# First expert layer by token halves, its weights by column halves, and two transfers of the second chunk moved

## The chip, the cores and the metric

The kernel runs on one core of one Trainium2 chip. The metric is the device time of the program in microseconds (us). Times are quoted as medians of all runs of a kernel, of the fast ones alone where one was slow. A ratio is the mean time of one kernel's fast runs over that of the other kernel's fast runs of the same rounds, so it is not quite the ratio of the medians. Positions in time below are in us from the start of the profiled span, which is some 1.7 us shorter than the time of the same run.

## The reference, cut to what matters

Four sequences of 768 tokens pass a gated linear attention with 8 heads of 48 channels. The result, 3072 rows of 384, passes four small two-layer experts whose outputs are mixed with given probabilities.

```python
state = np.zeros((B, H, D, D))
for t in range(S):
    state = f[:, :, t, :, None] * state + np.einsum('bhd,bhe->bhde', k[:, :, t], v[:, :, t])
    y[:, :, t] = np.einsum('bhd,bhde->bhe', q[:, :, t], state)
...
p = domain_probs / (domain_probs.sum(-1, keepdims=True) + 1e-09)
for e in range(E):                       # E = 4, w1: 384 x 1024, w2: 1024 x 384
    h = np.maximum(x @ w1[e], 0.0)
    out += p[:, e:e + 1] * (h @ w2[e])
```

## The kernel before

The sequence is cut into six chunks of 128 tokens, numbered c = 0 to 5 (the text also says "second chunk" for c = 1); a chunk holds 4 batches, so 512 rows of the expert part. All work is put down as small operations with an assumed cost for one or more engines, a priority number, dependencies, and the buffers they take and free. A planner in the kernel runs through assumed time and hands out operations; the order in which it hands them out is the order in which the instructions are emitted, on every engine and on the queue of SyncE (SP), which issues the loads of the chunks, small copies, transposing copies and the stores. An engine takes its instructions in this order. The assumed costs set orders; they are not measured times. An eviction, below, is the copy of a matmul's result out of a PSUM bank (PSUM is the memory into which the matmuls write) into a buffer in SBUF, the working memory; the kernel reuses the bank only after it.

```python
rooms = {"ps_m": 4, "ps_t": 4, "f": 4, "q": 4, "k": 4, "v": 4, ..., "xT": 2, "h": 2, "o": 6}   # buffers
...
def load(c, nm, b, n):                     # f, k, q, v of batches b .. b+n-1 of a chunk
    ins[c, nm, b] = nc.sync.dma_start(...)
    if (c, nm, b) == (1, "f", 0):
        after(ins[c, nm, b], ins["w", 5])  # behind the sixth of eight weights
def load_w(i, e, which):                   # one weight, f32 in memory, bf16 in SBUF
    ins["w", i] = nc.gpsimd.dma_start(out=w[:, e], in_=r[e])
    if i == 0:
        after(ins["w", 0], ins[0, "q", B - 1])
...
def mm_h(c, e, fc, n0, n1):                # first layer, 128 of 1024 hidden columns
    for kk in range(KD):                   # KD = 3
        nc.tensor.matmul(out=..., lhsT=w1_sb[:, e, kk, fc*128:(fc+1)*128], rhs=tl("xT", c)[:, kk, n0:n1], ...)
def ev_o(c, e, nt, part, cols, eng):       # output of one expert times its probability, into an "o" tile
...
for c in range(C):
    u0 = unit[0]                           # running number of expert units, used as priority
    if c == 0:
        zip_units(hl(c, 0, 0, NT, ALL), [])            # 8 units of 512 rows
    ...
    if c + 2 < C:
        for half in range(2):
            for j, nm in enumerate("fkqv"):
                add_load(c + 2, nm, 2 * half, 2, u0 + 30 + 4 * half + j, deps=[wd[5]])
```

In the head, until the first expert matmul, filler matmuls on a tile named busy keep TensorE active. In the profiles, the matmuls that read xT and w_sb are the first layer of the experts, those that read w_sb and h the second; qk, QK, AT, y, yb belong to the attention; o is an output tile.

## Time and profile before

| | before |
|---|---|
| time, three runs first measured | 303.52 us (303.27 to 303.71) |
| span of the profile | 301.9 us |
| TensorE busy | 96% |
| first expert matmul starts | 23.86 us |
| last matmuls end | 298.40 us |

TensorE bounds the kernel. The page and the chain that show it stand in the prediction below. To see where TensorE loses time although it is "busy", I compared start to start: for each kind of matmul there is an interval at which it repeats when nothing is waited for (0.2158 us for 512 columns of the first layer, 0.1093 for 256, 0.1623 for the 384 of the second layer, 0.0555 for a transpose, and so on). The sum of these intervals over the program's order is the nominal work; what the trace needs beyond it between two matmuls is lost there. For the kernel before, start 23.86 + nominal 272.04 + lost 2.24 = 298.14, the start of the last matmul. This account is used for every run below.

### The profile page before, as it was taken

The numbers are of one execution on the slowest core, as the hardware profiler recorded it, in microseconds if no ns is written. First come the engines' busy times: TensorE is split into PE (matmuls) and PEld (weight loads), VectorE is DVE, ScalarE is ACT, GpSimd is POOL, SyncE is SP. The second block draws the span as 40 slices with busy tenths as digits, with TensorE's granted clock in tenths as the row PEclk, the third lists the DMA queues.
The fourth block names the chain that finished last, engine by engine and source line by source line (L and its number), as shares of the span: only waits on it lengthen the run. The fifth ranks groups of instructions, "written<-read, shape, count | busy, mean of one in ns | idle before, by whom it ended". The sixth has DMA issues, their size and how long they took to land.

```text
span 301.9 us, 5498 instructions
## 1 busy us (share of the span) xinstructions
PE 291.2 (96%) x2107; PEld 168.6 (56%) x2137; DVE 130.1 (43%) x249; ACT 171.2 (57%) x302; POOL 95.5 (32%) x158
## 2 busy tenths in 40 slices
PE   7889999999999999999999999999999999999995
PEld 5654555566775566556555555555555555555553
DVE  5674002788752574506464335453415342201223
ACT  4766664755767454777356585445475444465430
POOL 4386300316576047423334533522342000000000
PEclk9999999999999999999999999999999999999999
DMA  9999999991995669989699969201322201200003
GB/s 150 203 168 207 208 208 205 179 157 34 197 228 119 117 121 181 213 155 158 125 199 173 207 122 154 48 16 37 91 60 51 49 15 40 78 0 2 0 0 104
DMA packets 134222, 36.08 MB, mean 120 GB/s; under 512 B 125340, under 2 KB 132636, under 8 KB 134196
## 3 DMA queue, kind: packets, MB, share of 16 engines
q1 hardware_dynamic: 128400, 29.40, 54.7%
q0 software_dynamic: 5760, 6.29, 12.5%
q8 instruction: 16, 0.26, 0.4%
q14 instruction: 10, 0.08, 0.1%
q10 hardware_dynamic: 36, 0.05, 0.1%
HBM read 31.51 MB, written 4.72 MB: 120 GB/s over the span
## 4 chain that ended last, share of the span: by engine, by line
PE 78%; DMA 12%; SPq 5%; POOL 2%; issue 1%; DVE 1%; POOLq 0%; DVEq 0%
PE ps_m L363 37%; PE ps_m L351 34%; DMA w_sb<-in_moe_w_dram 8%; SPq L225 5%; DMA q<-in_q_dram 4%; PE ps_t L307 2%; POOL w_sb L232 1%; PE ps_t L322 1%; PE ps_t L318 1%; PE ps_t L328 1%; POOL qk L283 1%; PE ps_t L259 1%; DVE qk L283 1%; PE ps_t L292 1%; PE ps_t L347 0%
## 5 line engine op out<-in xcount | busy, mean ns | idle before, releaser
L359 ACT ACTIVATE h<-ps_m 128x512 bf16<-128x512 f32 (+1 forms) x170 | 97.9, 577 | 99.4 <-PE ps_m L351 92.5
L363 PE MATMUL ps_m<-w_sb,h 128*128 128x384 bf16 x776 | 152.7, 324 | 0.2
L351 PE MATMUL ps_m<-xT,w_sb 128*128 128x512 bf16 (+1 forms) x594 | 150.2, 362 | 2.1 <-DMA w_sb<-in_moe_w_dram 0.7
L363 PEld LDWEIGHTS <-h 128*128 128x128 bf16 x776 | 73.4, 98 | 57.4
L370 DVE SCALAR_TENSOR_TENSOR o<-ps_m,pn,o 128x384 f32<-128x384 f32 (+1 forms) x73 | 44.6, 611 | 109.2 <-PE ps_m L363 104.9
L351 PEld LDWEIGHTS <-w_sb 128*128 128x128 bf16 x624 | 59.9, 98 | 47.1 <-DMA w_sb<-in_moe_w_dram 0.8
L283 POOL TENSOR_TENSOR qk<-q,e 128x384 bf16<-128x384 f32 x18 | 21.5, 1196 | 62.3 <-ACT e L269 33.4
L342 POOL TENSOR_TENSOR Sf<-Sf,egs 48x192 f32<-48x192 f32 x40 | 20.4, 511 | 45.4 <-DVE Sf L335 43.4
L357 DVE TENSOR_SCALAR h<-ps_m 128x512 bf16<-128x512 f32 (+1 forms) x38 | 21.5, 576 | 28.5 <-PE ps_m L351 27.1
L311 DVE TENSOR_TENSOR AT<-ps_t,mask 128x512 bf16<-128x512 f32 x48 | 30.2, 683 | 8.3 <-PE ps_t L307 8.3
L283 POOL TENSOR_TENSOR qk<-k,e 128x384 bf16<-128x384 f32 x21 | 22.1, 1052 | 18.2 <-ACT e L271 11.1
L269 ACT ACTIVATE e<-ps_t 128x384 f32<-128x384 f32 x20 | 17.3, 863 | 3.2 <-PE ps_t L259 1.4
L335 DVE TENSOR_TENSOR Sf<-Sf,ps_t 48x192 f32<-48x192 f32 x40 | 14.0, 349 | 10.7 <-PE ps_t L328 10.1
L372 ACT ACTIVATE o<-ps_m,pn 128x384 f32<-128x384 f32 x22 | 12.8, 580 | 4.2 <-PE ps_m L363 3.4
L343 POOL CAST sb<-Sf 48x192 bf16<-48x192 f32 x40 | 13.6, 340 | 2.6
L583 PE MATMUL ps_m<-busy 128*128 128x256 bf16 x61 | 12.4, 334 | 1.3 <-DVE busy L140 1.3
L251 ACT ACTIVATE ex<-f 128x768 f32<-128x768 f32 (+1 forms) x14 | 10.5, 750 | 4.1 <-DMA f<-in_f_logit_dram 4.0
L271 ACT ACTIVATE e<-ps_t 128x384 f32<-128x384 f32 x24 | 12.7, 531 | 0.0
L221 POOL CAST vb<-v 128x384 bf16<-128x384 f32 x19 | 9.8, 538 | 7.4 <-DMA v<-in_v_dram 5.1
L322 PE MATMUL ps_t<-vb,AT 128*128 128x48 bf16 x192 | 11.4, 184 | 0.7 <-ACT vb L219 0.7
L322 PEld LDWEIGHTS <-AT 128*128 128x128 bf16 x192 | 10.0, 97 | 2.8 <-issue 1.0
L255 ACT ACTIVATE gp<-ex 128x768 bf16<-128x768 f32 (+1 forms) x14 | 10.5, 750 | 0.4
(54 smaller groups left out, 131.6 us busy)
## 6 DMA issues: line engine op xcount, KB each, us to landing
w_sb<-in_moe_w_dram POOLq DMA_DIRECT2D x8, 768.0 KB, 18.5
out_dram<-o SPq DMA_DIRECT2D x23, 192.0 KB, 2.2
f<-in_f_logit_dram SPq DMA_DIRECT2D x10, 384.0 KB, 4.2
k<-in_k_dram SPq DMA_DIRECT2D x10, 384.0 KB, 5.0
q<-in_q_dram SPq DMA_DIRECT2D x10, 384.0 KB, 6.3
v<-in_v_dram SPq DMA_DIRECT2D x10, 384.0 KB, 5.8
f<-in_f_logit_dram SPq DMA_DIRECT2D x4, 192.0 KB, 4.3
k<-in_k_dram SPq DMA_DIRECT2D x4, 192.0 KB, 4.2
```

The costliest lines, as they stand in the source:

```text
L225: ins[c, nm, b] = nc.sync.dma_start(out=tl(nm, c, b // 2)[:, hh(b, n), :], in_=srcs[nm][c, :, b * H:(b + n) * H, :])
L269: nc.scalar.activation(out=e[:, 0].rearrange("t (d h) -> t h d", d=D), in_=cs[:, 0:HD].rearrange("t (i r d) -> t r i d", r=2, d=D), func=A ...
L283: engines[eng].tensor_tensor(out=tl("qk", c, b)[:, j, :, 0:D].rearrange("t (i r) d -> t i r d", r=2), in0=tl("qk"[j], c, b // 2)[:, hh(b), ...
L311: nc.vector.tensor_tensor(out=tl("AT", c, b)[:, r].rearrange("s i t -> s (i t)"), in0=tl("A", c, b, r).rearrange("s i t -> s (i t)"), in1= ...
L322: nc.tensor.matmul(out=y[:, h * D:(h + 1) * D], lhsT=AT[:, r, i, :], rhs=vb[:, h, :], start=(c == 0), stop=True, skip_group_check=True)
L335: nc.vector.tensor_tensor(out=Sf[rows, b], in0=Sf[rows, b], in1=KV[rows, :, r, :], op=ALU.add)
L342: nc.gpsimd.tensor_tensor(out=Sf[rows, b], in0=Sf[rows, b], in1=eg, op=ALU.mult)
L351: nc.tensor.matmul(out=tl("hp", c, e, fc, n0)[:, n0:n1], lhsT=w1_sb[:, e, kk, fc * 128:(fc + 1) * 128], rhs=tl("xT", c)[:, kk, n0:n1], sta ...
L357: nc.vector.tensor_relu(out=dst, in_=src)
L359: nc.scalar.activation(out=dst, in_=src, func=AF.Relu)
L363: nc.tensor.matmul(out=tl("op", c, e, nt, part)[:, cols], lhsT=tl("h", c, e)[:, fc, nt * T:(nt + 1) * T], rhs=w2_sb[:, e, fc, cols], start ...
L370: nc.vector.scalar_tensor_tensor(out=o, in0=op, scalar=pe, in1=o, op0=ALU.mult, op1=ALU.add)
```

## The change

The intent: the first expert's first layer need not wait for all four batches of chunk 0 nor for the whole weight, so TensorE starts earlier; and chunk 1's keys and queries come earlier because the last weight stands back. The costs that the planner assumes for chunk 0 are set anew. The core of the diff (cuts marked):

```diff
+        for o in self.ops:
+            if o.name.split(" ")[-1].startswith("0.") and set(o.costs) & {"ACT", "DVE"}:
+                o.lag += 0.1
...
-        if (c, nm, b) == (1, "f", 0):
-            after(ins[c, nm, b], ins["w", 5])
+        if (c, nm, b) == (1, "f", 1):
+            after(ins[c, nm, b], ins["w", w_gate])
-    def load_w(i, e, which):
+    def load_w(i, e, which, cols):
-        ins["w", i] = nc.gpsimd.dma_start(out=w[:, e], in_=r[e])
+        ins["w", i] = nc.gpsimd.dma_start(out=w[:, e, :, cols], in_=r[e][:, :, cols])
+        if i == w_gate + 2:
+            after(ins["w", i], ins[1, "k", 0])
...
+    add_load(1, "f", 0, 1, -980, cost=0.1)
+    pieces = [(0, 1, slice(0, F // 2)), (0, 1, slice(F // 2, F))] + [...]
+    wd, w_gate = {}, len(pieces) - 3
...
-            p, d, half = slot(b0, 0) - 0.5, 0.54 if gran == 1 else 0.84, b0 // 2
+            p, d, half = slot(b0, 0) - 0.5, 0.43 if gran == 1 else 0.84, b0 // 2
... (seven more assumed costs of chunk 0)
-            zip_units(hl(c, 0, 0, NT, ALL), [])
+            for n0, n1, xs in ((0, N2, LO), (N2, NT, HI)):
+                zip_units(hl(c, 0, n0, n1, xs), [])
```

More of the change, by code (lines that the diff above doesn't have):

```diff
@@ L381, with add_load @@
     ld = {}
-    nw = [(0, 1), (1, 1), (0, 2), (2, 1), (1, 2), (3, 1), (2, 2), (3, 2)]
-    def add_load(c, nm, b, n, prio, deps=()):
-        op = P.add(f"ld {nm}{c}.{b}", {"DMA": 1.05 * n}, lambda e: load(c, nm, b, n), prio,
+    def add_load(c, nm, b, n, prio, deps=(), cost=None):
+        op = P.add(f"ld {nm}{c}.{b}", {"DMA": cost or 1.05 * n}, lambda e: load(c, nm, b, n), prio,
                    deps=deps, takes=[(nm, c, b // 2)], lag=2.0)
@@ L392 @@
         add_load(0, x[0], int(x[1]), 1, -1000 + i)
-    wd = {}
-    for i, (e, which) in enumerate(nw):
-        iss = P.add(f"w issue {i}", {"POOL": 0.9}, lambda _, i=i, e=e, which=which: load_w(i, e, which),
-                    -500 + i, deps=[ld[0, "q", B - 1]])
-        wd[e, which] = wd[i] = P.add(f"w {i}", {"DMA": 4.5}, lambda _: None, -500 + (0, 1, 2, 3, 4, 5, 101.5, 103.5)[i], deps=[iss], lag=2.0)
-    for half in range(2):
-        for j, nm in enumerate("fkqv"):
-            add_load(1, nm, 2 * half, 2, -400 + 4 * half + j, deps=[wd[5]])
+    add_load(1, "f", 0, 1, -980, cost=0.1)
+    pieces = [(0, 1, slice(0, F // 2)), (0, 1, slice(F // 2, F))] + [
+        (e, which, slice(0, F if which == 1 else Din)) for e, which in ((1, 1), (0, 2), (2, 1), (1, 2), (3, 1), (2, 2), (3, 2))]
+    wd, w_gate = {}, len(pieces) - 3
+    for i, (e, which, cols) in enumerate(pieces):
+        if i == w_gate + 2:
+            for x in ((1, "f", 1, 1), (1, "k", 0, 2), (1, "q", 0, 2), (1, "v", 0, 2)):
+                add_load(*x, -430 + len(ld), deps=wd[3, 1])
+        iss = P.add(f"w issue {i}", {"POOL": 0.8}, lambda _, i=i, x=(e, which, cols): load_w(i, *x),
+                    -500 + i, deps=[ld[0, "q", B - 1]] + ([ld[1, "k", 0]] if i > w_gate + 1 else []))
+        op = P.add(f"w {i}", {"DMA": 2.25 if i < 2 else 4.5}, lambda _: None,
+                   -500 + (0, 0.5, 1, 2, 3, 4, 5, 6, 111)[i], deps=[iss], lag=1.5)
+        wd[e, which] = wd.get((e, which), []) + [op]
+    for x in ((1, "f", 2, 2), (1, "k", 2, 2), (1, "q", 2, 2), (1, "v", 2, 2)):
+        add_load(*x, -400 + len(ld), deps=wd[3, 1])
     xdone, kvdone = {}, {}
@@ L408, in attention @@
         for b0 in range(0, B, gran):
-            p, d, half = slot(b0, 0) - 0.5, 0.54 if gran == 1 else 0.84, b0 // 2
+            p, d, half = slot(b0, 0) - 0.5, 0.43 if gran == 1 else 0.84, b0 // 2
             g1 = P.add(f"gate1 {c}.{b0}", {"ACT": d}, lambda e, b0=b0: gate1(c, b0, gran), p,
-                       deps=[ld[c, "f", b0]], takes=[("ex", c, b0)], frees=[("f", c, half)])
+                       deps=[ld[c, "f", b0 + i] for i in range(gran)], takes=[("ex", c, b0)], frees=[("f", c, half)])
             g2 = P.add(f"gate2 {c}.{b0}", {"ACT": d}, lambda e, b0=b0: gate2(c, b0, gran), p + 0.1,
@@ L423, in attention @@
                        deps=[G[b]], takes=[pt_("cs")], lag=0.2, frees=[("gp", c, half)])
-            ex = P.add(f"exps {c}.{b}", {"ACT": 0.98 if c else 1.0}, on(exps), s(0) + 0.1, deps=[cs],
+            ex = P.add(f"exps {c}.{b}", {"ACT": 0.98 if c else 0.82}, on(exps), s(0) + 0.1, deps=[cs],
                        takes=[("e", c, b)] + ([("egs", c, b)] if c == 0 else []), frees=[pt_("cs")])
@@ L427, in attention @@
                             frees=[("e", c, b)], lag=2.0) if c and more else None)
-            pe = {"DVE": 0.55} if c == 0 and b == B - 1 else {"DVE": 0.55, "POOL": 1.36} if c == 0 else {"DVE": 0.6, "POOL": 1.0} if c == 1 else {"POOL": 1.0}
+            pe = {"DVE": 0.47} if c == 0 and b == B - 1 else {"DVE": 0.47, "POOL": 1.36} if c == 0 else {"DVE": 0.6, "POOL": 1.0} if c == 1 else {"POOL": 1.0}
             qm = P.add(f"q {c}.{b}", pe, one(product, 0), s(4) - 0.2,
@@ L432, in attention @@
                        deps=[ex, ld[c, "k", b]], takes=[("qk", c, b)], frees=[("k", c, half), ("e", c, b)])
-            vb = P.add(f"v {c}.{b}", {"ACT": 0.52} if c + b == 0 else {"ACT": 0.52, "DVE": 0.36} if c == 0 else {"POOL": 0.5, "ACT": 0.52} if c == 1 else {"POOL": 0.5}, one(cast_v), s(4),
+            vb = P.add(f"v {c}.{b}", {"ACT": 0.42} if c + b == 0 else {"ACT": 0.42, "DVE": 0.28} if c == 0 else {"POOL": 0.5, "ACT": 0.52} if c == 1 else {"POOL": 0.5}, one(cast_v), s(4),
                        deps=[ld[c, "v", b]], takes=[("vb", c, b)], frees=[("v", c, half)])
@@ L440, in attention @@
                 parts = [(slice(0, 2), [tq, tk])] if c or b < B - 1 else [(slice(j, j + 1), [tj]) for j, tj in enumerate((tq, tk))]
-                et = [P.add(f"ev_tp {c}.{b}", {"DVE": 0.69, "ACT": 1.05} if len(parts) == 1 else {"DVE": 0.37, "ACT": 0.55},
+                et = [P.add(f"ev_tp {c}.{b}", {"DVE": 0.69, "ACT": 1.05} if c else {"DVE": 0.6, "ACT": 0.92} if len(parts) == 1 else {"DVE": 0.35, "ACT": 0.49},
                             lambda e, b=b, js=js: copy(e, tl("QK", c, b)[0:MP, js], tl("tp", c, b)[0:MP, js]), s(4) + 0.1,
@@ L461, in attention @@
             at, vb = AT_[b], VB[b]
-            eA = [P.add(f"ev_at{r} {c}.{b}", {"DVE": 0.7}, on(ev_at, r), s(7) + 0.1 + 0.1 * r, deps=[at],
+            eA = [P.add(f"ev_at{r} {c}.{b}", {"DVE": 0.7 if c else 0.62}, on(ev_at, r), s(7) + 0.1 + 0.1 * r, deps=[at],
                         takes=[("AT", c, b)], frees=[pt_("A", r)]) for r in range(2)]
@@ L468, in attention @@
             cs_ = lambda ks: slice(ks.start * 128, ks.stop * 128)
-            ey = [P.add(f"ev_y {c}.{b}", {"ACT": 0.48, "DVE": 0.56} if len(parts) == 1 else {"ACT": 0.4, "DVE": 0.4},
+            ey = [P.add(f"ev_y {c}.{b}", {"ACT": 0.48, "DVE": 0.56} if c else {"ACT": 0.4, "DVE": 0.47} if len(parts) == 1 else {"ACT": 0.3, "DVE": 0.36},
                         lambda e, b=b, ks=ks: copy(e, tl("yb", c, b)[:, cs_(ks)], tl("y", c, b)[:, cs_(ks)]), s(11) + 0.1,
@@ L477, in attention @@
                     xdone[c, b].append(
-                        P.add(f"ev_xt {c}.{b}", {"ACT": 0.48, "DVE": 0.4} if len(parts) == 1 else {"ACT": 0.36, "DVE": 0.3},
+                        P.add(f"ev_xt {c}.{b}", {"ACT": 0.48, "DVE": 0.4} if c else {"ACT": 0.4, "DVE": 0.3} if len(parts) == 1 else {"ACT": 0.3, "DVE": 0.25},
                               lambda e, b=b, ks=ks: copy(e, tl("xT", c)[:, ks, b * T:(b + 1) * T], tl("xp", c, b, ks.start)[:, ks]),
@@ L503, in add_h @@
         m = P.add(f"h {c}.{e}.{fc}.{n0}", {"PE": 0.645 * n / NT}, lambda _: mm_h(c, e, fc, n0, n1), p,
-                  deps=[wd[e, 1]] + [t for b in xs for t in xdone[c, b]], takes=[key], lag=0.2, frees=[("xT", c)])
+                  deps=(wd[e, 1] if (c, e) != (0, 0) else [wd[0, 1][fc * 2 // KF]]) + [t for b in xs for t in xdone[c, b]], takes=[key], lag=0.2, frees=[("xT", c)])
         hdone[c, e, fc, n0] = P.add(f"relu {c}.{e}.{fc}.{n0}",
@@ L518, in add_o @@
         m = omm[c, e, nt] = P.add(f"o {c}.{e}.{nt}.{half}", {"PE": 0.645}, lambda _: mm_o(c, e, nt, fcs, part, cols), p,
-                                  deps=d + [wd[e, 2], omm.get((c, e, nt))], takes=[key], lag=0.2, frees=[("h", c, e)])
+                                  deps=d + wd[e, 2] + [omm.get((c, e, nt))], takes=[key], lag=0.2, frees=[("h", c, e)])
         if half == 1 or by_cols:
@@ L567 @@
                 for j, nm in enumerate("fkqv"):
-                    add_load(c + 2, nm, 2 * half, 2, u0 + 30 + 4 * half + j, deps=[wd[5]])
+                    add_load(c + 2, nm, 2 * half, 2, u0 + 30 + 4 * half + j, deps=wd[3, 1])
     zip_units([], ol(C - 1, E - 1, ALL))
```

## The prediction

> **What bounds the kernel now.** I read the page first, then the chain of waits in order of time, then TensorE's timeline at the head, the DMA windows there, and the waits of the second chunk's stage.
>
> ```profile
> PE 291.2 (96%) x2107; PEld 168.6 (56%) x2137; DVE 130.1 (43%) x249; ACT 171.2 (57%) x302; POOL 95.5 (32%) x158
> ...
> PE   7889999999999999999999999999999999999995
> ```
>
> TensorE is busy nearly everywhere. The reader should distrust the 96% (ends are modelled, fillers count) and look at the first three digits: only the head and the tail have room. The head, on TensorE's timeline:
>
> ```profile
> 21.05 0.38 PE L322 MATMUL ps_t<-vb,AT 128*128 128x48 bf16 x8
> 21.28 0.60 PE L583 MATMUL ps_m<-busy 128*128 128x256 bf16 x4
> 22.02 0.53 PE L347 MATMUL ps_t<-ident,yb 128*128 128x128 bf16 x3
> 22.39 0.60 PE L583 MATMUL ps_m<-busy 128*128 128x256 bf16 x4
> 22.82 0.33 PE L328 MATMUL ps_t<-vb,qk 128*128 128x96 bf16 x4
> 23.86 1.47 PE L351 MATMUL ps_m<-xT,w_sb 128*128 128x512 bf16 x5 [0.70 <-DMA w_sb<-in_moe_w_dram]
> ```
>
> The first expert matmul (the line of xT and w_sb) starts at 23.86 after 0.70 us of waiting for its weight. From there to the last matmul (292.52 + 5.88 = 298.40 in the chain) TensorE has 274.5 us. I tested how full that is with the instruction order: a 512-wide expert matmul takes 0.216 us and a 384-wide second-layer one 0.1625 (units of 3 and of 4 in the timeline both repeat every 0.65), a 256-wide one 0.109 (21 in 2.29). From 23.86 to the second chunk's first cumulative sum at 55.72 stand 84 x 0.216 + 80 x 0.1625 + 0.5 for three groups of state matmuls = 31.6; elapsed 31.9. So it is packed. The same count over all of the order gives 272.65, so 1.9 us is lost, and by comparing positions: 0.2 before 55.72, about 1.0 between 55.72 and 63.8, 0.6 to 0.7 between 68.5 and 77. Nothing after. Those two, and the 23.86, are all that this change can win.
>
> The chain of waits shows how both hang on transfers:
>
> ```profile
> 16.32 4.25 POOL w_sb L232 x5
> 20.57 22.88 DMA w_sb<-in_moe_w_dram
> ...
> 43.47 0.37 SPq L225
> ...
> 43.89 5.15 SPq L225
> 49.04 0.04 issue
> 49.08 8.48 DMA q<-in_q_dram
> ...
> 57.73 2.94 POOL qk L283 x2
> 60.67 0.05 issue
> 60.72 0.40 PE ps_t L292 x4
> ```
>
> Weights are issued from 16.32, the sixth lands at 43.45, the second chunk's keys and queries are only then issued, the queries land at 57.56, and the product on GpSimd that needs them releases TensorE at 60.72. The weights' own row:
>
> ```profile
> DMA to landing us min/median/max: 7.5/18.5/30.4
> ```
>
> The first lands at 16.3 + 7.5 = 23.8, the last (issued 22.2) at 52.6. From the first to the sixth: (43.45 - 23.8) / 5 = 3.93 us per weight of 768 KB. From the sixth to the eighth, with the chunk's first loads beside them, 9.1 us instead of 7.9.
>
> **What the Trainium skill says.** "DMA: Bandwidth & Descriptors", section "Anatomy of one DMA — SWDGE (gpsimd) path", gives about 2.0 us fixed plus bytes over 436 GB/s. For the 1.57 MB that a weight reads as f32 that is 3.6 us of movement; the trace has 3.93. So halving a piece halves about 3.9 us, not the 3.6 us of the 7.5 that are fixed or lie behind earlier transfers. The same page, "Queues, rings and completion order", says that an engine alternates between queues by packet, not by byte. The trace agrees in its result: queue 1 moved 29.40 MB in 128400 packets, queue 0 6.29 MB in 5760, nearly five times as large, and the first 384 KB load issued at 43.47 fed its activation only at 53.95, when the last two weights were through. "TensorE: Matmul & The Clock Gate", section "Back-to-back issue gap", has N / 2.4 + 2.5 ns: 109 ns for 256 columns, as measured here, so two halves cost 0.218 against 0.216. It also gives an estimate of up to 131 ns for 512 in a sustained stream; the trace has 216, and decides.
>
> **The change part by part.**
>
> 1. First weight in two column halves, first layer's first expert in two token halves. The 24 matmuls of 512 columns become 48 of 256: 48 x 0.109 - 24 x 0.216 = +0.05 us. They no longer need the last batch's transposed output (evicted about 22.8) but only the first two batches' (done at 20.44) and the first half weight. In the order they now stand right behind the fourth batch's output matmuls, which ended about 21.4; so the weight sets the start. Landing: 23.8 - 3.93 / 2 = 21.85, plus up to 0.3 for the next point. First matmul: about 22.0. Four units (12 matmuls, 1.3 us) use the first half; behind the third stands the last batch's transpose (0.17), which before preceded the start. That is 1.5 us of work, to 23.5. The fifth unit needs the second half of the weight, which lands when the whole did, 23.8, plus the same 0.3, and plus nothing for the extra issue, which is hidden in the queue: 24.0. TensorE so waits some 0.5 us in the middle of the first layer. At 24.0 it has 1.5 us of its count behind it; the kernel before had 0.14 at that point, and its 0.17 of first state matmuls. In the new order the count from the first expert matmul is 273.04 (transpose and state matmuls are now in it), so 273.04 - 1.47 = 271.57 remain at 24.0, against 272.65 - 0.14 = 272.5 before. **Gain 0.9 us**; had the second half been there too, 23.86 + 272.65 - 22.0 - 273.04 = 1.5.
>
> 2. The second chunk's first forget-gate tile (192 KB) is now loaded at the end of the first chunk's loads, before the weights fill the queue. It falls into stretches where the DMA engines had little:
>
> ```profile
> 17.00:17.50 0.50, 0.43 (x13) 0.27 (x8) 0.50 (x3) 0.22 (x1) 0.50 (x2) 1.00 0.19 32
> ...
> 19.00:19.50 0.50, 0.50 (x11) 0.34 (x10) 0.50 (x2) 0.42 (x1) 0.50 (x1) 1.00 0.74 94
> ```
>
> (last columns: DMA share and GB/s). 192 KB at 200 GB/s is 1 us, and I count 0.7 us of it as filling those holes, so the 0.3 above.
>
> 3. The last weight waits for the second chunk's first keys. After the seventh piece, 43.5 + 0.3, one weight, not two, stands before the small packets: 3.9 us to 47.7. Then the second gate tile (1.05), keys (2.1), queries (2.1, from the 2.05 us between issues in the steady part): gates near 49.5, keys near 51.5, queries near 54. That is 3.5 us before the 57.56 of now. The last weight, issued at 52, comes by about 59; it is first read at 39.1 in the count, some 62 us, so it isn't missed. What is won: the 0.2 before 55.72 and the 0.73 us for which GpSimd's first product waited past its exponentials (57.0 to 57.73). But GpSimd still does its two products of 1.3 and 1.6 us, and the exponentials' chain still starts from the cumulative sum, with the same distance to the transposes in the order (2.9 us). New GpSimd order: both are key products, whose exponentials are 0.35 us later than the query's. So of 1.2 us lost I give back 0.2 + 0.35: **gain 0.5**.
>
> 4. New cost numbers in the planner change the first chunk's order on ScalarE and VectorE (a transposed copy goes to ScalarE, others back), and 10 filler matmuls fall away (61 to 51). These fill gaps and are worth nothing themselves. I give 0.
>
> Sum: 0.9 + 0.5 = 1.4 us, less nothing at the tail, which is unchanged: 303.5 - 1.4 = 302.1.
>
> **The rivals.**
>
> - *The weight is not halved in time.* If both halves advance together, or the gate tile delays them by its whole 1 us, the second half lands at 24.8, and the head gains only 0.1: 303.0. For it: packets alternate. Against it: the landings of whole weights step by 3.93, in order.
> - *The wait moves to the second half of the second chunk.* TensorE arrives 1.4 us earlier, and the last weight now competes with the second half's loads. Its products start at 70.1, released by an exponential and not by a transfer; its loads were all issued by 63.4. In the new order its transposes stand 2.6 us behind the cumulative sum, not 2.9. If that costs 0.7: 302.8.
> - *The second stage gives everything.* If queries had been the whole cause of the 1.2 us, and the weight halves come earlier than I think, 2.4 to 2.7 us go: 301.0.
> - *Start set by attention.* If the new first-chunk order delays the fourth batch's output matmuls past 22, the earlier weight is for nothing: 303.
>
> **Range and chances.** The head gives between 0.1 and 2.0 (the latter if it starts at 21.4 and never waits), the second stage between -0.7 and 1.2. The ends don't come together: 300.9 to 303.3 around 302.1. Two per cent is 6.1 us; no part of this reaches it in either direction, since the 249 us of expert matmuls are untouched.
>
> **What would show it.** First expert matmul near 22.0, with the weight as what ended the wait; a second wait of about 0.5 us for the weight between 23 and 24.3; 48 matmuls of 128x256 there; the second chunk's gate activation no longer waiting for its load; GpSimd's first product released by an exponential; a shorter wait of TensorE at its second chunk's transposes; the last matmul 1.4 us earlier. It is wrong if the first expert matmul still starts after 23, if the waits around 58 to 77 add up to more than now, or if the last weight is waited for near 62.

## The result, and the profile after

| | before | after |
|---|---|---|
| time (4 runs each) | 303.56 us (303.27 to 303.71) | 307.15 us (306.55 to 308.93) |
| ratio to before, 95% interval | | 1.0129 (1.0083 to 1.0176) |
| span of the profile | 301.9 us | 304.8 us |
| first expert matmul starts | 23.86 us | 21.91 us |
| last matmuls end | 298.40 us | 301.41 us |

The kernel became 1.3% slower, clear of the noise, though within 2%: it starts its main work 1.95 us earlier and ends it 3.0 us later. The account by start to start, by stretches of the span (us):

| | start | nominal | lost to 50 | 50-65 | 65-88 | 88-100 | 100-160 | later | last matmul starts |
|---|---|---|---|---|---|---|---|---|---|
| before | 23.86 | 272.04 | 0.02 | 1.22 | 0.73 | 0.00 | 0.11 | 0.16 | 298.14 |
| after | 21.91 | 272.44 | 1.30 | 1.33 | 0.25 | 2.51 | 1.25 | 0.16 | 301.15 |

At 88 us the changed kernel is still ahead: -1.95 at the start, +0.40 of nominal work (24 extra matmuls, and two small groups that stood ahead of the start before), +1.28, +0.11 and -0.48 of losses, together -0.64. Then it loses 2.5 us at one place and 1.1 at two others, near 138 and 152 us.

The page's totals hardly show this. The rows that answer to those of before, and the group of the first layer's matmuls (last column: idle time ahead of them, and what ended most of it):

```profile
PE 288.8 (95%) x2121; PEld 169.1 (55%) x2151; DVE 132.1 (43%) x251; ACT 171.8 (56%) x308; POOL 96.0 (31%) x159
...
PE   7678999899996999999999999999999999999995
...
L356 PE MATMUL ps_m<-xT,w_sb 128*128 128x512 bf16 (+1 forms) x618 | 149.6, 354 | 5.4 <-ACT o L377 2.4
```

The busy share is only one point lower. The row of slices (7.6 us each) has one digit that stands out behind the head, the 6 in the thirteenth place, 91 to 99 us, and the group says what it may be: the first layer waited 5.4 us in all, 2.1 before, and 2.4 of them for an eviction on ScalarE. TensorE's timeline at the head shows the part that went as planned, and the first loss:

```profile
21.91 1.16 PE L356 MATMUL ps_m<-xT,w_sb 128*128 128x256 bf16 x9 [0.54 <-DMA w_sb<-in_moe_w_dram]
22.90 0.33 PE L352 MATMUL ps_t<-ident,yb 128*128 128x128 bf16 x3
23.07 0.49 PE L356 MATMUL ps_m<-xT,w_sb 128*128 128x256 bf16 x3
24.66 0.50 PE L356 MATMUL ps_m<-xT,w_sb 128*128 128x256 bf16 x3 [1.11 <-DMA w_sb<-in_moe_w_dram]
```

The first half of the weight lands at 21.86 and TensorE begins. After four units (3 + 1 in these rows) it waits 1.11 us for the second half, which lands at 24.62. The early gate tile is a likely reason: of SyncE's chunk loads it is the one that took longest to land, issued at 16.90 and landed at 28.07.

```profile
DMA to landing us min/median/max: 3.0/5.7/11.2
```

(us from issue to landing of the changed kernel's chunk loads.) It did not fit into the holes of the DMA engines; it was in flight beside the weights for 11.2 us.

The waits of TensorE from 85 to 100 us, where the kernel before has none at all:

```profile
PE ps_m L356 <- ACT o L377: 2.4, 1, 2.4
```

(columns: us in total, times, longest.) The chain of waits of the changed kernel says what that eviction itself waited for:

```profile
87.66 0.41 PE ps_m L368 x3
88.07 5.85 DMA out_dram<-o
93.92 0.02 issue
93.94 0.59 ACT o L377
94.53 0.04 issue
94.57 0.49 PE ps_m L356 x3
```

A matmul waits for a PSUM bank, the bank for an eviction on ScalarE into an output tile, the output tile for a store. There are six output tiles: chunk 0 holds four until they are stored, chunk 1's first expert takes two and then needs one back. The store was issued at 88.07 only. SyncE's queue in the kernel before:

```profile
76.96 2.08 SPq L225 DMA_DIRECT2D v<-in_v_dram  x1
79.13 2.81 SPq L378 DMA_DIRECT2D out_dram<-o  x1
81.99 0.43 SPq L225 DMA_DIRECT2D f<-in_f_logit_dram  x1
82.51 1.63 SPq L225 DMA_DIRECT2D k<-in_k_dram  x1
84.23 1.45 SPq L378 DMA_DIRECT2D out_dram<-o  x1
```

and in the changed kernel:

```profile
77.67 3.07 SPq L228 DMA_DIRECT2D v<-in_v_dram  x1
80.79 1.67 SPq L228 DMA_DIRECT2D f<-in_f_logit_dram  x1
82.57 1.92 SPq L228 DMA_DIRECT2D k<-in_k_dram  x1
84.58 1.72 SPq L228 DMA_DIRECT2D q<-in_q_dram  x1
86.35 1.62 SPq L228 DMA_DIRECT2D v<-in_v_dram  x1
88.07 2.54 SPq L383 DMA_DIRECT2D out_dram<-o  x2
```

The first store moved behind four more loads. The last sums into chunk 0's output tiles were done on VectorE between 66 and 72 us, so the stores were ready long before; they stood in line. From 77.67 on each load holds the queue for 1.6 to 3.1 us of issue; what sets this length was not tested.

Why they moved is arithmetic of the planner's numbers. A store's priority is the number of its expert unit; chunk 2's loads have the fixed numbers 30 to 37. The token halves make 16 units of the first 8, so the stores of chunk 0, which stood between the loads' numbers (33 and up), now have numbers from 41 on and rank behind all eight loads.

### The profile page after: what moved, and what is told of

Its sections match the earlier page's. It is cut to its first block, busy times and chain, and to the rows that moved or that the text cites.

```text
span 304.8 us, 5535 instructions
## 1 busy us (share of the span) xinstructions
PE 288.8 (95%) x2121; PEld 169.1 (55%) x2151; DVE 132.1 (43%) x251; ACT 171.8 (56%) x308; POOL 96.0 (31%) x159
## 4 chain that ended last, share of the span: by engine, by line
PE 80%; DMA 8%; SPq 5%; issue 3%; POOL 1%; ACT 1%; DVE 1%; POOLq 0%; ACTq 0%
PE ps_m L368 37%; PE ps_m L356 36%; SPq L228 3%; DMA w_sb<-in_moe_w_dram 2%; DMA out_dram<-o 2%; PE ps_t L312 2%; DMA f<-in_f_logit_dram 1%; DMA q<-in_q_dram 1%; PE ps_t L327 1%; PE ps_t L333 1%; DMA QK<-qk 1%; PE ps_t L323 1%; PE ps_t L264 1%; DVE qk L288 1%; SPq L301 1%
## 5 line engine op out<-in xcount | busy, mean ns | idle before, releaser
L356 PEld LDWEIGHTS <-w_sb 128*128 128x128 bf16 x648 | 62.0, 98 | 50.0 <-issue 2.8
L362 DVE TENSOR_SCALAR h<-ps_m 128x512 bf16<-128x512 f32 (+1 forms) x40 | 22.2, 562 | 32.2 <-PE ps_m L356 30.2
L288 POOL TENSOR_TENSOR qk<-q,e 128x384 bf16<-128x384 f32 x17 | 20.1, 1185 | 39.7 <-ACT e L274 35.4
L288 POOL TENSOR_TENSOR qk<-k,e 128x384 bf16<-128x384 f32 x22 | 23.2, 1056 | 23.2 <-ACT e L276 15.9
L235 POOL DMA_DIRECT2D w_sb<-in_moe_w_dram x9 | 7.6, 848 | 20.6 <-DMA k<-in_k_dram 18.3
L595 PE MATMUL ps_m<-busy 128*128 128x256 bf16 x51 | 9.5, 313 | 1.3 <-DVE busy L143 1.3
```

The lines of the kernel that those rows point to most:

```text
L288: engines[eng].tensor_tensor(out=tl("qk", c, b)[:, j, :, 0:D].rearrange("t (i r) d -> t i r d", r=2), in0=tl("qk"[j], c, b // 2)[:, hh(b), ...
L356: nc.tensor.matmul(out=tl("hp", c, e, fc, n0)[:, n0:n1], lhsT=w1_sb[:, e, kk, fc * 128:(fc + 1) * 128], rhs=tl("xT", c)[:, kk, n0:n1], sta ...
L362: nc.vector.tensor_relu(out=dst, in_=src)
```

## The experiments

Theory A: the output tile held by the late store is the main loss, and the token halves cause it through the numbering. Rival B: the DMA queue is late as a whole (more pieces, other order of loads), and the wait at 92 us only shows it. Beside these stood two smaller questions: what delays the second half of the weight, and why the earlier keys and queries of chunk 1 gained nothing between 50 and 65 us. Edits that move an emitted operation are made after planning, so every other engine keeps its order.

The account of all runs, in us by the same stretches (each from the profiled run):

| run | start | lost to 50 | 50-65 | 65-88 | 88-100 | 100-160 | last matmul starts |
|---|---|---|---|---|---|---|---|
| e1_obuf8 | 22.65 | 1.90 | 1.31 | 0.26 | 0.67 | 1.00 | 300.39 |
| e2_stores | 21.78 | 1.40 | 1.34 | 0.24 | 0.41 | 0.94 | 298.72 |
| e3_late | 23.88 | 0.02 | 1.29 | 0.73 | 1.42 | 0.12 | 299.67 |
| e4_tok | 23.36 | 0.02 | 1.14 | 0.78 | 1.36 | 0.11 | 299.05 |
| e5_f_late | 22.28 | 0.49 | 1.35 | 0.24 | 0.20 | 0.11 | 297.28 |
| e6_k3 | 22.41 | 0.49 | 1.35 | 0.24 | 0.39 | 0.12 | 297.61 |
| e7_w8_free | 22.08 | 1.29 | 1.42 | 0.25 | 0.45 | 0.28 | 298.38 |
| e8_numbers | 22.98 | 1.90 | 1.32 | 0.26 | 0.00 | 0.11 | 299.18 |
| e9_after | 22.91 | 2.02 | 1.31 | 0.27 | 2.60 | 0.12 | 301.84 |
| e10_repaired | 22.27 | 1.20 | 1.33 | 0.25 | 0.41 | 0.19 | 298.27 |
| e11_dve | 22.17 | 1.02 | 0.49 | 0.24 | 0.15 | 0.12 | 296.79 |
| e12_cols | 22.91 | 1.24 | 1.00 | 0.78 | 0.00 | 0.12 | 298.42 |

With the nominal work (272.0 to 272.4) and 0.2 us lost later, each row adds up to its last column.

On the later chips the time of one and the same kernel scatters by over 1 us (the kernel before: 303.42 to 307.08). One cause of the scatter is visible, at the end of this section.

### Eight output tiles

```diff
     done = P.run()
+    for c in range(C):
+        for nt in range(B):
+            P.slot["o", c, nt] = 4 * (c % 2) + nt
```

> The changed kernel with eight output tiles in place of six, given out by the parity of the chunk after planning, so every engine's order is unchanged. Theory A (a store of chunk 0 stands in the DMA queue behind eight loads and holds the output tile that chunk 1's third first-expert eviction needs): the wait of TensorE behind the eviction at 92 us (2.35 us idle, 2.5 us by start-to-start) is gone, and the time falls by at least 2.4 us, to 304.7 or less; if the two transposed-copy waits near 138 and 152 us (1.1 us together) are its consequence, by 3.6, to 303.5. Theory B (the store only shows a DMA queue that is late as a whole): the 2.5 us come back at the transposed copies, time 306.5 to 307.2.

Measured: 305.50 us (303.41 to 306.26), beside 304.14 for the kernel before on that chip; ratio 1.0025 (0.9975 to 1.0075). The wait behind the eviction is gone and the loss from 88 to 100 us fell from 2.51 to 0.67. One of the two waits for a transposed copy stayed (0.74 us near 151). So the tile was the wait, and the 2.5 us did not come back elsewhere: theory A in its size, though not in its hope that the copies would follow. The time itself missed what was expected by 0.8 us. The run's profile has a clock of 0.994 with TensorE at half clock from 22.56 to 25.97 us, right where the first layer begins: its 1.90 us up to 50 stand there. Its late start is another matter: the first half of the weight landed only at 22.61.

### The first two stores put ahead

```diff
     done = P.run()
+    move("store 0.0.0", "ld f2.2")
+    move("store 0.1.0", "ld q2.2")
```

(move takes an operation out of the emitted order and puts it before the other.)

> The changed kernel with its first two stores put ahead in the SP queue as they stand in the kernel before (behind v of chunk 2's first half, and behind k of the second); nothing else moves, six output tiles. Theory A: as with eight tiles, the wait at 92 us goes, time 303.3 to 304.7. Theory B: no more than 0.5 us is won.

Measured: 304.44 us (303.46 to 304.97); ratio to before 1.0004 (0.9974 to 1.0034). SyncE's queue of this run:

```profile
77.65 3.42 SPq L228 DMA_DIRECT2D v<-in_v_dram  x1
81.16 1.50 SPq L383 DMA_DIRECT2D out_dram<-o  x1
```

The store is issued 7 us earlier than in the changed kernel, with six tiles as before, and TensorE's only wait from 85 to 100 us is 0.2 us for another eviction. Loss there 0.41 for 2.51. Rival B expected no more than 0.5 us; 2.1 were won by moving two instructions. The time lies 0.1 us above the expected range.

### The stores put late in the kernel before

```diff
     done = P.run()
...
+    for name, behind in (("store 0.0.0", "ld v2.2"), ("store 0.1.0", "store 0.0.0")):
+        move(name, behind)
```

(here move puts it behind the other.)

> The kernel before with its first two stores moved behind all eight loads of chunk 2, as in the changed kernel; nothing else moves. Theory A: TensorE now waits there for 2 to 3 us behind an eviction that waits for a store, 305.5 to 306.5. Theory B (the cause is elsewhere in the change): 303.5, no such wait.

Measured: 306.20 us (304.80 to 307.70); ratio 1.0066 (1.0016 to 1.0116). The waits of TensorE and ScalarE that the kernel before did not have:

```profile
PE ps_m L351 <- ACT h L359: 0.5, 1, 0.5
PE ps_m L351 <- ACT o L372: 0.4, 1, 0.4
```

```profile
92.10 0.58 ACT L372 ACTIVATE o<-ps_m,pn 128x384 f32<-128x384 f32 x1 [2.66 <-DMA out_dram<-o]
```

(the first fence are waits of TensorE from 85 to 100 us, the second is a row of ScalarE's timeline.) The eviction again waits for the store, 2.66 us. TensorE loses 1.42 us there, less than the expected 2 to 3: its matmuls of chunk 1 stand 0.7 us later than in the changed kernel (the group of 21 at 85.94 for 85.20), and the store landed 1.9 us earlier (92.02 for 93.92), so part of the wait lay beside other work. Nothing else of the change is in this kernel. Theory A holds in this direction too.

### The token halves alone

```diff
-            zip_units(hl(c, 0, 0, NT, ALL), [])
+            for n0, n1, xs in ((0, N2, LO), (N2, NT, HI)):
+                zip_units(hl(c, 0, n0, n1, xs), [])
```

> The kernel before with the token halves of the first expert layer alone: whole first weight, loads and planner numbers as before. Its SP queue has both stores behind the eight loads, so theory A, with the order turned by the eight extra units of the numbering: wait of 2 to 3 us near 92, start at 23.9 as before, 305.5 to 307.5. Theory B (loads and weight pieces are what costs): 303.5 to 304.

Measured: 305.12 us (304.52 to 307.20); ratio 1.0042 (1.0000 to 1.0084). The two stores stand behind the eight loads in this kernel's order, and 1.36 us are lost from 88 to 100 us. The start came at 23.36, half a microsecond earlier than before, not unchanged as expected (the weight landed at 23.32 without an edit to its load, so landings can vary by this much from one profile to another); the loss is under the expected 2 to 3 us and the time 0.4 us below the range. Here the eviction that waits for the store is on VectorE, and TensorE waits 0.54 us behind it:

```profile
91.64 0.62 DVE L374 TENSOR_SCALAR o<-ps_m,pn 128x384 f32<-128x384 f32 x1 [1.36 <-DMA out_dram<-o]
92.31 0.81 PE L363 MATMUL ps_m<-w_sb,h 128*128 128x384 bf16 x4 [0.54 <-DVE o L374]
```

With the column halves, the early gate tile and the new planner numbers all out of play, the wait for the store is there: theory A. The token halves turned the queue. The rest of the 1.36 us are shorter waits from 90 us on, which were not traced to the store one by one.

### The early gate tile behind the first weight

```diff
 (as e2_stores)
+        if (c, nm, b) == (1, "f", 0):
+            after(ins[c, nm, b], ins["w", 1])
```

> As e2_stores, with the early gate tile of chunk 1 issued only when the second half of the first weight has landed; no engine's order moves. If the gate tile's packets take turns with the weight's and so delay the second half (24.64 in place of 23.8), the second half now lands at 23.8 to 24.0, TensorE's wait in the first layer falls from 1.4 us to 0.6, and the time falls by 0.7 to 0.8 against e2_stores. If instead the additional piece costs the 0.8 us by itself, the second half stays at 24.6 and the time is that of e2_stores.

Measured: 303.53 us (302.66 to 304.42); ratio to before 0.9965 (0.9917 to 1.0013). The head on TensorE's timeline:

```profile
23.44 0.49 PE L358 MATMUL ps_m<-xT,w_sb 128*128 128x256 bf16 x3
24.13 0.50 PE L358 MATMUL ps_m<-xT,w_sb 128*128 128x256 bf16 x3 [0.20 <-DMA w_sb<-in_moe_w_dram]
```

The second half lands at 24.08, 1.85 us behind the first half (22.23). In the changed kernel the two were 2.76 us apart. The gap between the halves is 2.46 to 2.99 us in all seven profiles with the early gate tile and the halved weight, and 1.85 to 1.94 in the four with the tile held back (this run, e6, e10, e11). So the gate tile costs 0.9 us between the two halves, and the extra piece by itself costs nothing to be seen. The wait shrank from 1.21 us in e2_stores to 0.20, the loss of the first layer from 1.40 to 0.49, as expected. The gain is not safe, though: in e10 and e11, with the same head, TensorE waits for the first expert's second-layer weight, which landed at 34.03 and 33.74 (33.03 here, 32.94 in the changed kernel), and loses 0.70 and 0.52 us near 34.

### Chunk 3's first keys between two transposing copies

```diff
 (as e5_f_late)
+    move("ld k3.0", "xt 2.1")
```

> As e5_f_late, and the first keys of chunk 3 stand between the two transposes of the hidden input, as in the kernel before. If that exchange in the SP queue causes the wait for the transposed copy near 150 us (0.83 us), it goes, and the time falls by 0.8 more; if it is a queue that is late as a whole, the wait stays.

Measured: 302.89 us (302.70 to 303.10); ratio 0.9944 (0.9901 to 0.9987). The wait for the transposed copy near 150 us is not there, but it was not there in e5_f_late either, whose queue still has the exchange. So this run decides nothing about it. The wait was in the first profile of the changed kernel, in e1 and in e2, and is missing in e5, in e7 and in the repeat of the changed kernel itself (e9: 0.12 us lost from 100 to 160). What brings these 0.7 to 1.1 us in some executions stays open.

### The last weight without its wait

```diff
 (as e2_stores)
-        if i == w_gate + 2:
-            after(ins["w", i], ins[1, "k", 0])
```

> As e2_stores, but the last weight doesn't wait for chunk 1's keys (it is issued near 33 us). Keys and queries of chunk 1 land later (53 to 57.5 for 51.3 and 53.5). Theory 1 (my prediction: earlier keys are worth some 0.5 us of TensorE near 58 to 61): time up by 0.5 or more against e2_stores. Theory 2 (GpSimd and VectorE now start their products together and slow each other, 1.63 us for 0.55, so the earlier keys win nothing): TensorE's loss between 55 and 62 stays near 1.1 us, time as e2_stores within 0.3.

Measured: 304.04 us (303.48 to 305.19); ratio 0.9986 (0.9938 to 1.0035), 0.4 us below the median of e2_stores on another chip. The keys of chunk 1 now land at 55.17 and the queries at 57.28, 3.8 us later than in the changed kernel, and TensorE loses 1.42 us from 50 to 65 us, against 1.34 in e2_stores. Theory 2: the earlier keys are worth under 0.1 us.

### The planner's number mended at its source

```diff
-                add_load(c + 2, nm, 2 * half, 2, u0 + 30 + 4 * half + j, deps=wd[3, 1])
+                add_load(c + 2, nm, 2 * half, 2, u0 + (30 if c else 38) + 4 * half + j, deps=wd[3, 1])
```

> The changed kernel with the planner's number of chunk 2's loads put up by the 8 units that the token halves add (30 to 38); the planner makes the order itself, and the stores stand as in the kernel before, other engines' orders move too. If the fixed number is the cause: no wait of TensorE behind the first expert's evictions near 92, and a loss in the trace of 4 to 5 us in place of 6.8, as in e2_stores.

Measured: 303.65 us (303.26 to 304.70); ratio 0.9965 (0.9913 to 1.0017). No wait of TensorE at all from 85 to 100 us; loss there 0.00, in total 3.76 (a little under the expected 4 to 5), although its first layer fell into a stretch of half clock. With the eight units added to the loads' numbers, the planner itself puts the stores where they were.

### The changed kernel once more, beside a repaired one

The first of the two has no edit; the second is e6_k3 again.

> The changed kernel once more, on the chip of the repaired ones. The wait behind the first expert's evictions near 92 us is there again (2 to 3 us), time 1.0 to 1.5 per cent above the kernel before.

> e6_k3 once more, beside the changed kernel: stores ahead, gate tile behind the first weight, keys of chunk 3 between the transposes. 0.3 to 0.8 per cent below the kernel before, and at least 3 us below the changed kernel.

Measured on one chip, five rounds: before 304.59 us, the changed kernel 307.36 (306.28 to 308.38 in its five fast runs; a sixth, of 311.48 at a clock of 0.983, is left out), ratio 1.0092 (1.0041 to 1.0144), and the repaired one 302.96 (302.45 to 304.17), ratio 0.9948 (0.9908 to 0.9988). The wait at 92 us is there again in the changed kernel (2.60 us). Its ratio is 0.1 points under the expected 1.0 to 1.5 per cent; the other expectations were met.

### Chunk 1's first products on one engine

```diff
 (as e10_repaired)
+    for o in done:
+        if o.name in ("k 1.0", "k 1.1"):
+            o.engine = "DVE"
```

> As e10_repaired, but the two key products of chunk 1's first half are on VectorE, so that its four products run one after the other and GpSimd does none beside them. If sharing with GpSimd is what slows VectorE's product from 0.55 to 1.63 us, the four take about 2.3 us in a row from 57 us, TensorE's loss between 55 and 62 us falls from 1.1 us to 0.5 or less, and the time by 0.3 to 0.6. If the products were slow for another reason (early operands, the layout of the queries' factors), four of them take over 4 us and TensorE loses 2 us more.

Measured: 302.12 us (301.39 to 303.29); ratio to before 0.9916 (0.9876 to 0.9956). How long the products take is shown by their source line from 55 to 62 us, first in the changed kernel, where GpSimd and VectorE start at the same moment, then here:

```profile
L288 POOL TENSOR_TENSOR qk<-k,e x2: 998/1280/1563, 57.0 to 58.0; 128x384 bf16<-128x384 f32 x2
L288 DVE TENSOR_TENSOR qk<-q,e x2: 1650/1664/1678, 57.0 to 58.6; 128x384 bf16<-128x384 f32 x2
```

```profile
L290 DVE TENSOR_TENSOR qk<-k,e x2: 548/554/560, 57.0 to 59.0; 128x384 bf16<-128x384 f32 x2
L290 DVE TENSOR_TENSOR qk<-q,e x2: 849/852/854, 57.5 to 58.2; 128x384 bf16<-128x384 f32 x2
```

(ns, shortest, median, longest.) A query product takes 0.85 us alone (the 0.55 of the expectation is a key product's) and 1.66 beside GpSimd. Side by side the two engines take turns: GpSimd's first product ends at 57.99, VectorE's first 0.71 us later (58.70), GpSimd's second 0.87 us after that (59.56), VectorE's second 0.71 us after that (60.27). All four in a row on VectorE end at 59.55 and the first pair at 58.3; split over two engines, the first pair was ready at 58.7 and the second at 60.3. TensorE's loss from 50 to 65 us fell from 1.33 to 0.49, and the time by 0.84 us against e10_repaired, more than the expected 0.3 to 0.6. So it is mainly the engines' collision, not the arrival of the keys, that set this stage. In the kernel before, the late queries had kept the engines apart in part: VectorE began its first product, one of keys, at 57.49 while GpSimd still waited for the transfer until 57.73, and needed no more than its 0.55 us. The Trainium skill, "SBUF — State Buffer", section "SBUF: two separate sides", says that VectorE and GpSimd share a pair of ports that one of them holds for a whole instruction, also when VectorE reads two inputs from SBUF; the turns here agree with it. This kernel is faster than the kernel before and the changed one.

### Everything but the token halves

```diff
-            for n0, n1, xs in ((0, N2, LO), (N2, NT, HI)):
-                zip_units(hl(c, 0, n0, n1, xs), [])
+            zip_units(hl(c, 0, 0, NT, ALL), [])
```

> The changed kernel without the token halves (column halves, loads and planner numbers as changed). Its SP queue has the stores as in the kernel before. If the token halves alone turned the queue, no wait behind the evictions near 92 us, and the time is within 0.5 per cent of the kernel before, 2.5 to 4 us below the changed kernel; its first expert matmul starts only when the fourth batch's transposed output is evicted, at 22.7 to 23.

Measured: 303.67 us (303.16 to 304.52); ratio 0.9967 (0.9928 to 1.0006), 3.7 us below the changed kernel by the medians of the fast runs of the same rounds (expected 2.5 to 4). The stores stand as in the kernel before, no wait of TensorE between 85 and 100 us, start at 22.91; 1.21 of its 1.24 us up to 50 are lost at 33.22, where the second layer waits for its weight. Together with e4_tok and e8_numbers this closes the chain: with the token halves the loss is there, without them it isn't, and eight added to a number takes it away.

### The scatter

The changed kernel spread over more than 2 us in its first four runs (clock 1.0 in two profiles, 0.994 and 0.989 in the others). The stretches of the repeat's head show it (last columns: granted clock, DMA share, GB/s):

```profile
22.00:24.00 2.00, 1.09 (x11) 0.99 (x12) 0.23 (x1) 0.38 (x1) 0.84 (x1) 0.99 1.24 202
24.00:26.00 2.00, 1.49 (x10) 0.83 (x9) 1.38 (x6) 0.57 (x2) 0.00 (x0) 0.50 1.13 210
26.00:28.00 2.00, 2.00 (x21) 1.73 (x20) 1.65 (x6) 0.77 (x2) 0.80 (x2) 0.66 1.15 206
```

A clock of 0.99, 0.50 and 0.66 over 2 us each is 0.04 + 2.0 + 1.36 = 3.4 us at half speed. The Trainium skill, "TensorE: Matmul & The Clock Gate", section "What's actually happening", says that the clock is halved or freed by windows of 3413 ns that run free of the kernel's start; 3.4 us agrees. The stretch fell at 22 to 28 us in e1, e8 and e9, where it slows expert matmuls, and at 14 to 18 us in e2, e3 and e12, where it slows only the head. In e1, e8 and e9 the first half of the weight had also landed later, at 22.61 to 22.93 (21.73 to 22.36 in the eight other profiles with column halves); which of the two brings the other, if either, is not shown. Whether the changed kernel, with 51 fillers for 61, falls into half clock more often was not tested: its clock was under 0.995 in 7 of 10 runs, that of the kernel before in 10 of 25 runs, too few to tell.

## Why the prediction was wrong, by its own steps

**The bound and the start.** That TensorE is packed, and that an earlier start is worth its length, was right: first expert matmul predicted at 22.0, measured 21.91; first half of the weight at 21.85, measured 21.86. That the two agree to 0.01 us is luck, since this landing varied from 21.73 to 22.93 in the eleven profiles with column halves. The 3.6 us of movement per weight that it works out from the skill's page is an estimate; the landings gave its 3.93. The nominal work grew by 0.40, as counted.

**The second half and the gate tile.** Right in mechanism, wrong in size. The prediction gave the second half 24.0 and TensorE 0.5 us of waiting; it landed at 24.62 and cost 1.28 us. The term that failed is the 0.3 us for the gate tile, "I count 0.7 us of it as filling those holes". The tile landed at 28.07, long after those holes, and cost 0.9 us between the halves (e5_f_late). The passage on packets in the Trainium skill, "DMA: Bandwidth & Descriptors", "Queues, rings and completion order", cited in the same text, had pointed there, and so had the first rival. The head gained about 0.3 us (1.95 - 0.40 - 1.28), not 0.9.

**The keys and queries.** Their times were right (51.5 and 54 predicted, 51.32 and 53.45 measured), the gain of 0.5 us was not: between 50 and 65 us the loss went from 1.22 to 1.33. The step that failed followed GpSimd alone ("GpSimd still does its two products of 1.3 and 1.6 us") and left out the query products, which now stood on VectorE. GpSimd was indeed done earlier (59.56 for 60.66), but VectorE, set free at the same moment, had to take turns with it and was done only at 58.70 and 60.27, and TensorE's waits there are for VectorE (e7_w8_free, e11_dve). From 65 to 88 us, 0.48 us came back that the prediction had not claimed, so the sum of both stages, 0.37, was near its 0.5 by luck. Why they came back is open: e4_tok, with the token halves alone, and e12_cols, with all but them, both lost 0.78 us there.

**What put the time outside the range** is the sentence "Nothing after. Those two, and the 23.86, are all that this change can win", read as if nothing after could be lost. The prediction speaks of the new orders on TensorE, GpSimd, ScalarE and VectorE, but of SyncE's queue, 129 operations of the plan, only up to chunk 1's loads. Behind them, two stores had changed places with four loads, the first that frees an output tile was issued at 88.07 us for 79.13 before, and no rival named an output tile. By the account this is 2.5 us; with it, the head's size and the second stage as measured, and without the 1.1 us of transposed copies, the changed kernel would have been predicted at 303.5 - 0.27 - 0.37 + 2.51 = 305.4 us. The copies' 1.1 us and half-clock stretches make up the rest to 307.15, the median of the runs; the first of these is not explained. None of its three signs of being wrong came true (start at 21.91, not after 23; 1.58 us lost from 50 to 88 us, not more than the 1.95 of before; no wait for the last weight): it looked for trouble only where it expected the gain.

**The planner's new costs.** Given as worth 0. No run took them away alone, so this stands untested; e4_tok shows only that the main loss does not need them.

## What to carry to other kernels

Where one planner orders all queues by a running number, splitting a piece of work renumbers everything behind it; so compare the order of every queue, that of loads and stores too, and look for fixed offsets. A store frees a buffer, so a store that stands behind loads which nobody needs yet can stop the matmuls, here for 2.5 us: give stores the earliest place at which their data is ready, or more buffers. And an operand that comes earlier gains nothing if it makes two engines start at the same moment that have to take turns, as VectorE and GpSimd did here.

## What the Trainium skill lacked or had wrong

- "DMA: Bandwidth & Descriptors", "Queues, rings and completion order": it says that queues take turns by packet, but not what that does to a load of small pieces beside large ones. Here a load of 192 KB in runs of 192 bytes, issued beside the weights, took 11.2 us to land (7.8 to 12.0 in the seven profiles that have it), and lengthened the gap between two half weights by 0.9 us; the medians of the other kinds of load of 192 KB in the changed kernel are 4.2 to 5.3 us.
- The same page, "Issuing engines are not separate DMA queues", calls the sequencer's time to initiate a DMA usually small relative to the DMA itself. On SyncE's queue the issue of the queries at 49.08 in the kernel before took 4.46 of the 8.5 us to their landing, and in the changed kernel eight loads in a row held back a store that was ready for some 14 us (73.78 to 88.07). The page does not tell how much may be in flight before the issue itself waits.
- "TensorE: Matmul & The Clock Gate", "Back-to-back issue gap": its 131 ns per matmul of 512 columns in a sustained stream was not seen; at full clock every stretch of the traces has 216, which is the page's figure for the isolated case, and 109 for 256 columns.
- "SBUF — State Buffer", "SBUF: two separate sides": it says that one engine blocks the other, but has no figures for products of two f32 inputs on both at once. Here VectorE's query product took 0.85 us alone and 1.65 to 1.69 beside GpSimd's.
